# New set places for the attention and word steps of a fused attention and two-layer expert kernel

## The chip, the cores and the metric

The kernel runs on 1 core of one Trainium2 chip. The metric is device time in microseconds (us), the median of several executions. TensorE is called PE, VectorE DVE, ScalarE ACT, GpSimd POOL; SP is the engine whose queue issues nearly all transfers here.

## The reference, cut to what matters

```
scores = q @ k^T / sqrt(64)          # 4 batches, 8 heads, 576 positions, window of 64
attn   = softmax over the window
x      = attn @ v                    # 2304 tokens x 512
a, b   = x @ w1, x @ w2              # 512 -> 1024
h      = (a * b) @ w3 @ w_out        # 1024 -> 1024 -> 512
g      = leaky_relu(h @ w_in)        # 512 -> 2048
out    = g @ w_out2                  # 2048 -> 512
```

The weights arrive as 64-bit floats. "Word" stands below for one unit of 128 x 512 weights that is brought from 64 to 32 bits and then split.

## The kernel before, in words

Every large product is made of three fp32r products of high and low halves (`mm3`). The program has a first part written slot by slot, and a second part that a scheduler lays out.

**Slots.** From the start to the end of batch 2 the order on every engine is the order of the code (`Strict.on`). `slot()` issues, for the running slot number, first the attention work for PE (`ev["pe"]`), then one `ab_step`, which is 12 matmuls `ab` of 288 columns, then the eviction of the slot before, and then the other engines' work (`ev["post"]`) by rank. The first 13 slots (`HEAD`) have no `ab_step`: they hold the attention of batch 0. Batch b then takes 32 slots (`START[b]` and on), beside which the attention of batch b+1 runs. Even products are copied by ACT (`io<-ab`), odd ones multiplied on DVE (`p<-ab,io`).

**A pair.** Attention goes in 24 pairs, six to a batch: `prep` transposes q and k on DVE (six pieces for every three pairs), `scores` are 48 small matmuls `mm` on PE, `maxima` six fused operations on DVE (`s<-mm,mask`) with their read-outs, `exps` six on ACT, `normal` a sum and a product on POOL with a reciprocal on DVE between them, `turn` six transposes on PE (`mm<-ident,s`), `turned` their copies to `pts` (on DVE for batch 0, on ACT after that), `av` 24 matmuls `pa`, and then x is split by ACT (`x_hi`) and DVE (`x_lo`). `PAIRS` has the slot t of each pair's scores, and `plan()` sets the rest by fixed distances: exps at t+1, normal at t+2, turn at t+4, av at t+5, `x_lo` at t+6, with hh=1 one slot later in batch 0. Scores of a pair of batch 1 to 3 take all four banks of `ps_mm`; a turn takes two of them.

**A word.** `advance` moves four words on by one step each: scale and low bits on ACT (`f<-raw`, `low<-raw`), shift and the joining of bits on DVE (`f<-f,low`, `f<-raw,f`), then the cast to the high half on ACT (`w<-f`) and the low half on POOL (w1, w2) or DVE (the others). The load of word n+4 is queued on SP when word n's bits are joined (`feed`). Words of w1 and w2 are taken in slots 1 to 31, those of w_in and w_out beside batches 1 and 2. The rest (w3, and half of w_in) comes with batch 3.

**Fold.** Beside batch 3, w3 @ w_out is made once: a word of w3 is transposed on PE (`pa<-ident,f`), split (`w3T`), and multiplied (`mm<-wf,w3T`, 512 columns). Words of w_in are written out to DRAM by `keep` (`wd<-f`) from the buffer `f`, of which there are four for words of w3 and w_in together. From 380 us on, the remaining products run.

Of the kernel before, what the change touches and what calls it, by code (L numbers as in the profile page):

```python
# [21 lines left out]
def tile_kernel(ctx: ExitStack, tc: tile.TileContext, q, k, v, w1, w2, w3, w_out, w_in, w_out2, out):  # L22
# [18 lines left out]
    P = 128  # L41
# [18 lines left out]
    RAW = 4  # L60
    HEAD = 13
    LEAD = 13
# [105 lines left out]
    def load(ls):  # L168
        for dst, src in ls:
            sp.dma_start(dst, src)  # L170
# [154 lines left out]
    def low_bits(u):  # L325
        n_of["low"] += Strict.on
        u["low"] = (att if n_of["low"] % 2 else stage).tile([P, UC], I32, name="low", tag="low", bufs=1)
# [3 lines left out]
    def advance(stop):  # L331
# [12 lines left out]
        if now["fin"] < now["bits"]:  # L344
            u = units[now["fin"]]
            u["fin"](u["f"])
            n_of["fin"] += 1
# [127 lines left out]
    def plan():  # L475

        done = {}
        for b in range(B):
            order = [(2 * b + quad, gr) for quad in range(2) for gr in range(NG)]
            if b == 0:  # L480
                order = [(quad, gr) for gr in range(NG) for quad in range(2)]
            for (m, gr), t in zip(order, PAIRS[b]):
                at(t, 3 if b else 0, scores, m, gr, pe=True)
                for hh in range(2):
                    g = (m, hh, gr)
                    at(t, 3, maxima, g)
                    at(t + 1 + (0 if b else hh), 4, exps, g)
                    at(t + 2 + (0 if b else hh), (0, 6.5)[hh] if b else 0, normal, g)
                    at(t + (4 if b else 3 + hh), 1, turn, g, pe=True)
                    at(t + (4 if b else 3 + hh), 1, turned, g)  # L490
                    at(t + 5, 2, av, g, pe=True)
                    at(t + 5, 2, x_hi, g)
                    at(t + 6, 1, x_lo, g)
                    done[2 * m + hh] = t + 5
                if gr == 0:
                    for i in range(2 * EP):
                        if m == 1:
                            at(i // 3, 2 if i < 2 else 5, prep, m, i)
                        elif m:
                            at(t - 3 + i // 2, 5, prep, m, i)  # L500
                    if 2 <= m < 2 * B - 2:
                        at(t + 1, 7, lambda m: load(loads_qk(m)), m + 2)
# [4 lines left out]
        for t in [1, 3, 5, 7, 9, 10, 11, 13, 14, 15, 16, 17, 19, 21, 23, 25, 27, 29, 31]:  # L507
            at(t, 6, advance, PHASE_B)
        for b, stop in ((1, WO_FROM), (2, W3_FROM)):
            for i, t in enumerate(PAIRS[b + 1]):  # L510
                for d in (0, 2, 4) if i % NG < 2 else (0, 4):
                    if t + d < START[b] + 4 * KF:
                        at(t + d, 6, advance, stop)

# [13 lines left out]
    def start_loads():  # L528

        todo = [x for n in range(NHP) for x in loads_v(n)]  # L530
        for m in range(2):
# [15 lines left out]

    def ab_step(b, hf, f, j):
        cs = slice(NH * hf, NH * hf + NH)
        p, c = divmod(f, 2)  # L550
# [15 lines left out]
    def b_out(b, hf, p, c, ps, a):  # L566
        if c == 0:
            prods[p, hf] = gp.tile([P, 2, NH], F32, name="p32", tag="p32", bufs=4)
        p32 = prods[p, hf][:, c]
        with nullcontext() if Strict.on else first():  # L570
            dve.tensor_tensor(out=p32, in0=ps, in1=a, op=ALU.mult)
        if c and hf:
            p1, p2 = (prods.pop((p, i)) for i in range(2))
# [9 lines left out]
            later(3, lambda: sp.dma_start(pb[b][:, 4, p], t3))  # L583
        elif c:
            p1 = prods[p, hf]
            later(1, lambda: sp.dma_start(pb[b][:, 0:2, p], p1))
# [247 lines left out]
    for b in range(B):  # L834
        if b == 0:
            seq = [(hf, f) for fs in (range(0, 4), range(4, 8)) for hf in range(2) for f in fs]
        else:
            seq = [(hf, f) for p in range(KF // 2) for hf in range(2) for f in (2 * p, 2 * p + 1)]
# [403 lines left out]
```

## Time and profile before

| | us |
|---|---|
| median of 3 executions | 831.95 (831.71 to 832.5) |
| the profiled execution, its own time | 833.16 |
| span of the profiled execution | 831.4 |
| PE busy | 788.5 (95%) |
| DVE busy | 611.8 (74%) |
| ACT busy | 456.7 (55%) |
| POOL busy | 101.3 (12%) |

The span is from the first to the last instruction of one execution; its own time has the launch around it too. A busy share is a mean over stages with different limits, so the stages are read apart: the head and batches 0 to 2, to 272 us; batch 3 with the fold, to 380 us; and the rest. In a row of the timeline the bracket at the end is the idle time of the engine before that row, and who ended it.

### The profile page before, as it was taken

How to read it: one execution, taken by the hardware profiler on the slowest of the kernel's cores; microseconds unless marked ns; L12 is line 12 of the kernel's file. 1: busy time of each engine (PE TensorE's matmuls, PEld its weight loads, DVE VectorE, ACT ScalarE, POOL GpSimd, SP SyncE). 2: the span in 40 equal slices, each digit the busy share in tenths (PEclk: the TensorE clock that was granted, in tenths of full speed). 3: DMA queues.
4: the chain of work that ended last, by engine and by line, in shares of the span. 5: the costliest groups of instructions: out<-in, count | busy, mean ns of one | idle time of the engine just before them, and what ended most of it. 6: DMA issues, size and time to landing. Idle time of an engine off the chain costs nothing.

```text
span 831.4 us, 18254 instructions
## 1 busy us (share of the span) xinstructions
PE 788.5 (95%) x6856; PEld 761.0 (92%) x6856; DVE 611.8 (74%) x1446; ACT 456.7 (55%) x1103; POOL 101.3 (12%) x149
## 2 busy tenths in 40 slices
PE   3768999999989989999999999999999999999998
PEld 3557899999989978989999999999999999999997
DVE  5986636845882866758788886877667999798976
ACT  2866545544644424426556655555556766665744
POOL 1544622333222000000000000000000000000000
PEclk9979999999999999999999999999999999999999
DMA  9649547684461666535666356998898755343321
GB/s 273 210 117 307 181 129 185 192 257 113 128 190 45 222 187 193 180 103 158 199 191 213 121 190 218 313 332 306 307 340 270 241 190 160 102 153 125 106 96 57
DMA packets 121545, 157.97 MB, mean 190 GB/s; under 512 B 42736, under 2 KB 82928, under 8 KB 121456
## 3 DMA queue, kind: packets, MB, share of 16 engines
q1 hardware_dynamic: 121312, 156.66, 60.4%
q8 instruction: 54, 0.88, 0.4%
q14 instruction: 35, 0.29, 0.1%
q10 hardware_dynamic: 144, 0.13, 0.0%
HBM read 104.07 MB, written 52.69 MB: 189 GB/s over the span
## 4 chain that ended last, share of the span: by engine, by line
PE 72%; DVE 11%; DMA 9%; issue 3%; POOL 2%; ACT 2%; SPq 0%; DVEq 0%; ACTq 0%; POOLq 0%
PE pr L76 28%; PE o L76 22%; PE ab L78 12%; PE mm L78 5%; DMA wd<-f 4%; DVE f L76 2%; PE pa L78 2%; DMA raw<-in_moe_w_dram 2%; PE ab L76 2%; DVE f L78 2%; POOL s L78 1%; PE mm L76 1%; DVE s L78 1%; DMA vt<-in_v_dram 1%; DVE x L78 1%
## 5 line engine op out<-in xcount | busy, mean ns | idle before, releaser
L78 PE MATMUL ab<-x,w 128*128 128x288 f32 x1152 | 165.7, 301 | 0.0
L76 PE MATMUL pr<-yop,w 128*128 128x384 f32 x900 | 161.1, 337 | 0.0
L78 PEld LDWEIGHTS ab<-x,w 128*128 128x128 f32 x1152 | 156.5, 191 | 3.6 <-issue 3.2
L76 PEld LDWEIGHTS pr<-yop,w 128*128 128x128 f32 x900 | 157.4, 188 | 1.0 <-ACT c L76 0.9
L76 PE MATMUL o<-yop,yop 128*128 128x256 f32 x777 | 94.9, 282 | 0.0
L76 PEld LDWEIGHTS o<-yop,yop 128*128 128x128 f32 x777 | 93.6, 190 | 0.0
L76 ACT COPY c<-pr 128x384 f32<-128x384 f32 x95 | 45.1, 478 | 61.7 <-PE pr L76 55.0
L76 ACT CAST yop<-raw 128x256 fp32r<-128x256 f32 (+2 forms) x116 | 54.4, 491 | 38.3 <-PE o L76 34.5
L76 DVE TENSOR_TENSOR yop<-raw,yop 128x256 fp32r<-128x256 f32 (+2 forms) x116 | 58.2, 525 | 16.4 <-ACT yop L76 15.9
L78 ACT ACTIVATE s<-s,nm 128x128 f32<-128x128 f32 x144 | 56.0, 393 | 19.2 <-DVE nm L78 19.2
L76 ACT CAST yop<-f 128x512 fp32r<-128x512 f32 (+2 forms) x102 | 54.9, 567 | 20.1 <-DVE f L76 15.3
L76 DVE TENSOR_TENSOR yop<-f,yop 128x512 fp32r<-128x512 f32 (+2 forms) x102 | 59.3, 618 | 4.5 <-ACT yop L76 4.5
L76 DVE TENSOR_TENSOR c<-pr,c 128x384 f32<-128x384 f32 x74 | 40.8, 554 | 28.2 <-PE pr L76 15.6
L78 DVE CUSTOM_DVE_ANT_0 s<-mm,mask 128x128 f32<-128x128 f32 x144 | 32.2, 286 | 33.8 <-PE mm L78 33.8
L76 PEld LDWEIGHTS ab<-x,w 128*128 128x128 f32 x384 | 53.5, 189 | 1.8
L76 PE MATMUL ab<-x,w 128*128 128x288 f32 x384 | 55.1, 296 | 0.0
L76 PE MATMUL mm<-wf,w3T 128*128 128x512 f32 x192 | 52.3, 409 | 2.5 <-ACT w3T L76 2.5
L78 DVE TENSOR_TENSOR p<-ab,io 128x288 f32<-128x288 f32 x48 | 21.7, 453 | 36.2 <-PE ab L78 17.3
L78 ACT COPY io<-ab 128x288 f32<-128x288 f32 x48 | 19.1, 399 | 51.3 <-PE ab L78 51.2
L76 ACT ACTIVATE f<-raw 128x512 f32<-128x512 f32 x40 | 26.6, 674 | 35.4 <-DMA wd<-f 28.0
L76 PE MATMUL o<-w,yop 128*128 128x256 f32 x378 | 45.9, 282 | 0.0
L78 POOL TENSOR_TENSOR s<-s,rs 128x384 f32<-128x384 f32 x48 | 41.2, 858 | 36.2 <-DVE rs L78 34.3
(121 smaller groups left out, 1371.9 us busy)
## 6 DMA issues: line engine op xcount, KB each, us to landing
hd<-c SPq DMA_DIRECT2D x96, 192.0 KB, 4.1
raw<-hd SPq DMA_DIRECT2D x32, 512.0 KB, 3.7
raw<-in_moe_w_dram SPq DMA_DIRECT2D x28, 512.0 KB, 5.1
raw<-in_moe_w_out_dram SPq DMA_DIRECT2D x24, 512.0 KB, 5.1
pb<-p SPq DMA_DIRECT2D x32, 288.0 KB, 4.4
raw<-in_moe_w_in_dram SPq DMA_DIRECT2D x16, 512.0 KB, 4.0
wd<-f SPq DMA_DIRECT2D x32, 256.0 KB, 4.5
raw<-wd SPq DMA_DIRECT2D x30, 256.0 KB, 4.7
```

Source lines behind the costliest of these rows:

```text
L76: return f(*a, **k)
L78: r = f(*a, **k)
```

## The change

- A table `PLAN` replaces the distances written in `plan()`. It has a slot for every pair and, for each batch, the distances of exps, normal, turn, av and `x_lo`, each of the six transposes' slots, the slots of word steps, and those of three loads. In batch 0 pair 5 moves from slot 10 to 11. The turn of batch 3's pairs comes 5 slots behind the scores, where it was 4, the av 6 behind in batches 1 and 3; exps of the first half come in the slot of the scores.
- `turned` goes to ACT for all pairs.
- Of the 16 words of w1 and w2, five have no low bits from ACT (`low` 0): DVE masks them (`TENSOR_SCALAR f<-f`) and joins the low bits in one more operation. Eight are cast on DVE (`cast` 1).
- q and k of the first quad are loaded in three pieces each.
- Words of w_in that come among those of w3 get two buffers `fk` of their own, and two words of w3 are begun before batch 3.
- `THIRDS` is False, so its branches do nothing.

```diff
-    HEAD = 13
+    PLAN = {'head': 13, 'thirds': False, 'pairs': [[0, 2, 4, 6, 8, 11], [5, 7, 12, 19, 22, 27], [1, 6, 11, 18, 21, 27], [1, 5, 9, 15, 19, 25]], 'lags': [[1, 2, 2, 3, 3, 4, 5, 6], [0, 1, 2, 2, 4, 4, 6, 7], [0, 1, 2, 2, 4, 4, 5, 6], [0, 1, 2, 2, 5, 5, 6, 7]],
...
-        (act.copy if g[0] > 1 else dve.tensor_copy)(pts, grp[g])
+        (act.copy if PLAN["turned"][g[0] > 1][g[1]] else dve.tensor_copy)(pts, grp[g])
...
-            act.copy(t[:, 0, sl], f)
+            n = n_of["fin"]
+            (dve.tensor_copy if n < PHASE_B and PLAN["cast"][n] else act.copy)(t[:, 0, sl], f)
...
-            u["f"] = stage.tile([P, UC], F32, name="f", tag="f", bufs=4)
+            u["f"] = p0.tile([P, UC], F32, name="fk", tag="fk", bufs=2) if "own" in u else stage.tile([P, UC], F32, name="f", tag="f", bufs=4)
...
-                if now["scale"] < PHASE_B:
+                if now["scale"] < PHASE_B and PLAN["low"][now["scale"]]:
...
-        for m, t in ((2, 3), (3, HEAD + 4)):
+        for m, t in zip((2, 3), PLAN["loads"]):
...
-            at({4: 16, 5: done[0] + 1, 6: done[1] + 1}.get(n, done[n - 3] + 1), 7, lambda n: load(loads_v(n)), n)
+            at(max(PLAN["loads"][2], done[n - 3] + 1 if n > NHP else 0), 7, lambda n: load(loads_v(n)), n)
...
-            load(loads_qk(m))
+            ls = loads_qk(m)
+            load([(t[:, n * i:n * i + n], s[:, n * i:n * i + n]) for t, s in ls for i in range(EP)] if m == 0 else ls)
...
-            until(W3_FROM, W3_FROM)
+            while n_of["fin"] < W3_FROM or n_of["bits"] < W3_FROM + 2:
+                advance(W3_FROM + 2, W3_FROM)
```

On PE, the end of the head and the first slots with products, before, from the scores of pair 5 to the first scores of batch 1 (`kT` or `x` at 64x128):

```order
L78 MATMUL mm<-x 64x128 x24
L78 MATMUL mm<-ident,s 128x128 x6
L78 MATMUL pa<-pts,wf 64x64 x12
L78 MATMUL mm<-ident,s 128x128 x6
L78 MATMUL pa<-pts,vt 64x64 x12
L78 MATMUL ab<-x,w 128x288 x12
L78 MATMUL mm<-ident,s 128x128 x3
L78 MATMUL ab<-x,w 128x288 x12
L78 MATMUL pa<-pts,wf 64x64 x12
L78 MATMUL ab<-x,w 128x288 x24
L78 MATMUL mm<-kT,qT 64x128 x24
```

The same place after, from the turn that follows those scores:

```order
L79 MATMUL mm<-ident,s 128x128 x3
L79 MATMUL pa<-pts,wf 64x64 x12
L79 MATMUL mm<-ident,s 128x128 x3
L79 MATMUL pa<-pts,vt 64x64 x12
L79 MATMUL ab<-x,w 128x288 x12
L79 MATMUL mm<-ident,s 128x128 x3
L79 MATMUL ab<-x,w 128x288 x12
L79 MATMUL mm<-ident,s 128x128 x3
L79 MATMUL ab<-x,w 128x288 x12
L79 MATMUL pa<-pts,wf 64x64 x12
L79 MATMUL ab<-x,w 128x288 x24
L79 MATMUL mm<-kT,qT 64x128 x24
```

Both turns of pair 5 now stand behind the first `ab`, and five `ab` steps stand ahead of batch 1's first scores, where there were four.

On SP, the loads of words 8 to 13 (`raw`) and of v for batch 1 (`vt`, two rows a tile), before:

```order
L78 DMA raw_652<-in_moe_w1_dram 128x2x256
L78 DMA raw_717<-in_moe_w1_dram 128x2x256
L78 DMA raw_752<-in_moe_w2_dram 128x2x256
L78 DMA vt_754<-in_v_dram 128x9x64
L78 DMA vt_754<-in_v_dram 128x8x64
L78 DMA vt_757<-in_v_dram 128x9x64
L78 DMA vt_757<-in_v_dram 128x8x64
L78 DMA raw_802<-in_moe_w2_dram 128x2x256
L78 DMA raw_830<-in_moe_w1_dram 128x2x256
L78 DMA vt_832<-in_v_dram 128x9x64
L78 DMA vt_832<-in_v_dram 128x8x64
L78 DMA raw_896<-in_moe_w1_dram 128x2x256
```

After, the loads of words 8 to 14 and the first of those of v behind them:

```order
L79 DMA raw_590<-in_moe_w1_dram 128x2x256
L79 DMA raw_662<-in_moe_w1_dram 128x2x256
L79 DMA vt_664<-in_v_dram 128x9x64
L79 DMA vt_664<-in_v_dram 128x8x64
L79 DMA raw_688<-in_moe_w2_dram 128x2x256
L79 DMA raw_761<-in_moe_w2_dram 128x2x256
L79 DMA raw_796<-in_moe_w1_dram 128x2x256
L79 DMA raw_835<-in_moe_w1_dram 128x2x256
L79 DMA raw_860<-in_moe_w2_dram 128x2x256
L79 DMA vt_862<-in_v_dram 128x9x64
L79 DMA vt_862<-in_v_dram 128x8x64
```

Two of the three tiles of v went behind word 14; one went ahead of word 10.

On ACT, the first words of the fold, before (`f` is the scaled word, `w3T` the cast of a transposed one, `io` the copy of a product):

```order
L76 CAST w3T_4090<-pa_4091 128x512
L76 ACTIVATE f_4103<-raw_4086 128x512
L76 COPY io_4295<-ab_4282 128x288
L76 ACTIVATE f_4118<-raw_4101 128x512
L76 COPY io_4360<-ab_4347 128x288
L76 CAST w3T_4105<-pa_4106 128x512
L76 ACTIVATE f_4149<-raw_4116 128x512
L76 ACTIVATE f_4187<-raw_4124 128x512
L76 CAST w3T_4151<-pa_4152 128x512
L76 ACTIVATE f_4202<-raw_4162 128x512
```

After:

```order
L77 CAST w3T_4090<-pa_4091 128x512
L77 COPY io_4221<-ab_4208 128x288
L77 ACTIVATE f_4147<-raw_4114 128x512
L77 COPY io_4293<-ab_4280 128x288
L77 ACTIVATE fk_4200<-raw_4160 128x512
L77 CAST w3T_4100<-pa_4101 128x512
L77 ACTIVATE f_4185<-raw_4145 128x512
L77 COPY io_4358<-ab_4345 128x288
L77 ACTIVATE fk_4322<-raw_4263 128x512
L77 CAST w3T_4149<-pa_4150 128x512
```

Of the scaled words, those of w_in, every third of the stage, went from `f` to `fk`.

## Rows read from the trace of the kernel before

**Rows 1.** The page's head: the span.

```profile
span 831.4 us, 18254 instructions
```

**Rows 2.** PE's waits, 48 to 100 us: total us, times, longest.

```profile
PE mm L78 <- DVE qT L78: 4.1, 1, 4.1
PE mm L78 <- POOL s L78: 3.8, 4, 1.3
...
```

**Rows 3.** PE's waits, 100 to 272 us.

```profile
PE mm L78 <- POOL s L78: 3.6, 5, 1.3
PE pa L78 <- DMA vt<-in_v_dram: 0.8, 1, 0.8
PE mm L78 <- DVE qT L78: 0.7, 1, 0.7
```

**Rows 4.** PE's timeline: start, us, instructions, idle before.

```profile
45.53 0.90 PE L78 MATMUL mm<-ident,s 128*128 128x128 f32 x3 [2.59 <-DVE pts L78]
...
47.84 3.25 PE L78 MATMUL ab<-x,w 128*128 128x288 f32 x12
...
61.66 1.76 PE L78 MATMUL mm<-kT,qT 32*64 32x128 f32 x48 [4.09 <-DVE qT L78]
63.35 7.49 PE L78 MATMUL ab<-x,w 128*128 128x288 f32 x48
```

**Rows 5.** Chain that ended last, one undisturbed pair in batch 0.

```profile
106.74 0.65 PE mm L78 x6
...
108.98 0.85 PE pa L78 x24
109.83 1.07 PE mm L78 x48
110.90 6.58 PE ab L78 x48
```

**Rows 6.** Timeline of DVE and POOL in the head.

```profile
4.36 2.34 DVE L78 STREAM_TRANSPOSE kT<-x 128x384 f32<-128x384 f32 x3 [4.36 <-DMA x<-in_k_dram]
...
11.90 0.29 DVE L78 CUSTOM_DVE_ANT_0 s<-mm,mask 128x128 f32<-128x128 f32 x1 [1.61 <-PE mm L78]
...
19.15 0.29 DVE L78 CUSTOM_DVE_ANT_0 s<-mm,mask 128x128 f32<-128x128 f32 x1 [2.92 <-PE mm L78]
...
41.95 1.71 POOL L78 TENSOR_TENSOR w<-f,w 128x512 fp32r<-128x512 f32 x1
42.46 1.75 DVE L78 SCALAR_TENSOR_TENSOR f<-f,low 128x512 int32<-128x512 int32 x1
44.42 0.61 DVE L78 TENSOR_TENSOR x<-pa,x 128x192 fp32r<-128x192 f32 x2
...
48.74 0.68 DVE L78 SCALAR_TENSOR_TENSOR f<-f,low 128x512 int32<-128x512 int32 x1
```

**Rows 7.** DVE's groups, shapes apart, 0 to 272 us: busy, mean ns, idle before.

```profile
L78 DVE CUSTOM_DVE_ANT_0 s<-mm,mask 128x128 f32<-128x128 f32 x144 | 32.2, 286 | 33.8 <-PE mm L78 33.8
...
L78 DVE SCALAR_TENSOR_TENSOR f<-f,low 128x512 int32<-128x512 int32 x16 | 15.2, 948 | 0.0
...
L78 DVE TENSOR_SCALAR f<-f 128x512 int32<-128x512 int32 x16 | 9.1, 569 | 0.0
...
L78 DVE COPY pts<-mm 128x384 f32<-128x384 f32 x12 | 6.6, 547 | 2.6 <-PE mm L78 2.6
```

**Rows 8.** ACT's timeline in batch 0, the longest wait for a word.

```profile
66.92 0.67 ACT L78 ACTIVATE f<-raw 128x512 f32<-128x512 f32 x1 [5.01 <-DMA raw<-in_moe_w_dram]
```

**Rows 9.** SP's timeline: the loads of v inside those of words.

```profile
55.72 5.47 SPq L78 DMA_DIRECT2D vt<-in_v_dram  x4
```

**Rows 10.** Timeline of PE and ACT in the fold.

```profile
281.16 2.00 PE L76 MATMUL mm<-wf,w3T 128*128 128x512 f32 x8
...
295.93 0.66 ACT L76 ACTIVATE f<-raw 128x512 f32<-128x512 f32 x1 [7.42 <-DMA wd<-f]
...
297.12 3.50 PE L76 MATMUL mm<-wf,w3T 128*128 128x512 f32 x8 [2.47 <-ACT w3T L76]
```

More of the change, by code (lines that the diff above doesn't have):

```diff
@@ L60, in tile_kernel @@
     RAW = 4
-    HEAD = 13
+    PLAN = {'head': 13, 'thirds': False, 'pairs': [[0, 2, 4, 6, 8, 11], [5, 7, 12, 19, 22, 27], [1, 6, 11, 18, 21, 27], [1, 5, 9, 15, 19, 25]], 'lags': [[1, 2, 2, 3, 3, 4, 5, 6], [0, 1, 2, 2, 4, 4, 6, 7], [0, 1, 2, 2, 4, 4, 5, 6], [0, 1, 2, 2, 5, 5, 6, 7]], 'first': [0, 3, 3, 0], 'late': [[0, 4.5], [0, 0], [0, 6.5], [0, 9]], 'turns': [[0, 0, 0, 1, 1, 1], [10, 12, 15, 15, 16, 16], [25, 25, 28, 28, 30, 30], [41, 41, 43, 43, 45, 45], [56, 56, 58, 59, 62, 62], [72, 72, 73, 74, 76, 77], [86, 87, 88, 88, 89, 90]], 'turn_rank': 2, 'loads': [3, 19, 11], 'turned': [[1, 1], [1, 1]], 'words': [[0, 1, 3, 5, 7, 9, 10, 11, 12, 14, 15, 16, 17, 19, 23, 24, 26, 28, 28], [5, 6, 8, 9, 14, 14, 19, 20, 23, 23, 24], [2, 3, 4, 5, 8, 12, 14, 16, 17, 20, 20, 23, 25, 27, 27, 32, 33]], 'low': [1, 1, 1, 0, 1, 0, 1, 1, 1, 1, 1, 0, 0, 0, 1, 0], 'cast': [1, 1, 1, 1, 0, 1, 1, 0, 0, 0, 0, 0, 0, 0, 1, 1]}
+    HEAD, THIRDS = PLAN["head"], PLAN["thirds"]
     LEAD = 13
@@ L326, in low_bits, with advance @@
         n_of["low"] += Strict.on
-        u["low"] = (att if n_of["low"] % 2 else stage).tile([P, UC], I32, name="low", tag="low", bufs=1)
+        u["low"] = (att if Strict.on and n_of["low"] % 2 else stage).tile([P, UC], I32, name="low", tag="low", bufs=1)
         act.activation(out=u["low"], in_=flat(u["raw"]).bitcast(U8).rearrange("p (m e) -> p m e", e=8)[:, :, 3],
                        func=AF.Copy, scale=1.0 / 32, bias=-31.0 / 64)
-    def advance(stop):
+    def advance(stop, fins=None):
         now = dict(n_of)
@@ L460, in tile_kernel @@
             in_unit(8 + i // 2)
+            units[-1]["own"] = True
     n_of["cap"] = KEPT = len(units)
@@ L481, in plan @@
                 order = [(quad, gr) for gr in range(NG) for quad in range(2)]
-            for (m, gr), t in zip(order, PAIRS[b]):
-                at(t, 3 if b else 0, scores, m, gr, pe=True)
+            t0 = START[b - 1] if b else 0
+            for i, (m, gr) in enumerate(order):
+                t, lag = t0 + PLAN["pairs"][b][i], PLAN["lags"][b]
+                at(t, PLAN["first"][b], scores, m, gr, pe=True)
                 for hh in range(2):
@@ L495, in plan @@
[L495 to L500, printed above, removed]
+                    at(t + lag[hh], 4, exps, g)
+                    at(t + lag[2 + hh], PLAN["late"][b][hh], normal, g)
+                    at(t + lag[4 + hh], 1, turn, g, pe=True)
+                    at(t + lag[4 + hh], 1, turned, g)
@@ L501, in plan @@
+                    at(t + lag[6], 2, av, g, pe=True)
+                    at(t + lag[6], 2, x_hi, g)
+                    at(t + lag[7], 1, x_lo, g)
+                    done[2 * m + hh] = t + lag[6]
+                if gr == 0 and m:
+                    for k in range(2 * EP):
+                        at(PLAN["turns"][m - 1][k], PLAN["turn_rank"] if m == 1 else 5, prep, m, k)
                     if 2 <= m < 2 * B - 2:
-                        at(t + 1, 7, lambda m: load(loads_qk(m)), m + 2)
@@ L509, in plan @@
[L509 to L513, printed above, removed]
+            at(max(PLAN["loads"][2], done[n - 3] + 1 if n > NHP else 0), 7, lambda n: load(loads_v(n)), n)
+        for b, stop in enumerate((PHASE_B, WO_FROM, W3_FROM)):
+            for t in PLAN["words"][b]:
+                at((START[b] if b else 0) + t, 6, advance, stop + (2 if b == 2 else 0), stop)
@@ L548, in ab_step @@
     def ab_step(b, hf, f, j):
+        NH = S // (2 if b or not THIRDS else 3)
         cs = slice(NH * hf, NH * hf + NH)
@@ L566, in b_out @@
     def b_out(b, hf, p, c, ps, a):
[L567 to L572, printed above, removed]
+        for i, at_, n, n0 in ((((0, 0, 192, 0),), ((0, 192, 96, 0), (1, 0, 96, 96)), ((1, 96, 192, 0),))[hf] if b == 0 and THIRDS else ((hf, 0, NH, 0),)):
+            if (p, i) not in prods:
+                prods[p, i] = gp.tile([P, 2, NH], F32, name="p32", tag="p32", bufs=4)
+            with nullcontext() if Strict.on else first():
+                dve.tensor_tensor(out=prods[p, i][:, c, at_:at_ + n], in0=ps[:, n0:n0 + n], in1=a[:, n0:n0 + n], op=ALU.mult)
+        if c and hf == (1 if b or not THIRDS else 2):
             p1, p2 = (prods.pop((p, i)) for i in range(2))
@@ L583, in b_out @@
             later(3, lambda: sp.dma_start(pb[b][:, 4, p], t3))
-        elif c:
-            p1 = prods[p, hf]
+        elif c and hf == (0 if b or not THIRDS else 1):
+            p1 = prods[p, 0]
             later(1, lambda: sp.dma_start(pb[b][:, 0:2, p], p1))
@@ L835, in tile_kernel @@
         if b == 0:
-            seq = [(hf, f) for fs in (range(0, 4), range(4, 8)) for hf in range(2) for f in fs]
+            seq = [(hf, f) for fs in (range(0, 4), range(4, 8)) for hf in range(3 if THIRDS else 2) for f in fs]
         else:
```

18 lines of the change are left out of this document (4 added, 14 removed).

## The prediction

> **What bounds the kernel now.** I read the busy shares in slices first. Behind 380 us PE is busy in nearly every slice; nothing there is touched, so that part should only move. Everything changed lies ahead of 380 us. I then read PE's waits by stretch [rows 2, 3], PE's timeline at the places where they fall [rows 4], and the chain of waits for what an undisturbed pair costs [rows 5]: 0.65 + 0.85 + 1.07 us for turn, av and scores, and 6.58 us for four slots of products, 1.65 us a slot. Between the first product at 47.84 us [rows 4] and the end of batch 2 near 272 us stand 96 such slots (158 us), 18 whole pairs (46 us) and about 2 us left of batch 0: 206 us of work in 224 us. The 18 us between are what a better order can reach: 7.9 us of waits in the listed rows to 100 us and 5.1 us behind that [rows 2, 3], and low clock after idle time. In the head PE mostly waits, and DVE and ACT do the work one behind the other. In the fold a single wait of 2.47 us and its aftermath stand out [rows 10].
>
> **The head.** Up to the low half of x for the fourth pair, which batch 0's first product needs, the order has this on DVE: nine copies to pts fewer, four casts, two masking operations and two two-input operations on words more, and one transposition more. By the means of [rows 7] the copies give back 9 x 0.547 = 4.9 us. The added ones cost 2 x 0.95 + 2 x 0.57 = 3.0 us, and the transposition 2.34 / 3 = 0.8 us [rows 6]. A DVE cast of 512 columns has no row; the nearest is the one-input masking operation, 0.57 us, with the two-input 0.95 us as the upper bound and its undisturbed 0.68 us [rows 6] between; below 0.4 us it can hardly go. I take 0.57: 2.3 us. Net: DVE gets 1.2 us more (0.5 to 2.7). Against it stand gaps that the order now fills. The first transpositions waited for the whole of k until 4.36 us [rows 6]; with three pieces the first can start earlier, worth 0 to 1.5 us (DVE's own 2.34 us is the limit), I take 0.7. The third transposition of quad 1 falls into the idle 1.61 us before the first maxima: 0.7 us. A shift falls into the 2.92 us before the next ones [rows 6]: 0.6 us. So DVE is ready about 0.8 us earlier than 44.42 + 0.61 = 45.0 us. But PE did not start then: the turn of pair 5 stood ahead, after 2.59 us of waiting for DVE's pts [rows 4], then an av. Both turns of pair 5 now stand behind the first product, and the copies are on ACT. With the av of pair 4 still ahead I put the first product at 45.3 us: **-2.5 us** (0 to -4.0). Two things must hide for that. The first word's scale now leads ACT's queue, and the second stands between the two halves' exps of pair 0; each waits for its load, with those exps behind it. The cover is the second pair's scores and the turn of the second half, far behind; without it the wait is bounded by the longest one for a word, 5.0 us [rows 8].
>
> **Batch 0, to 100 us.** The 4.09 us for qT [rows 4] go if the six transpositions of quad 2 are done: the order starts them in slots 10 and 12, not 14, and the scores come one slot later. The pairs' other 3.8 us are turns behind POOL's product. Its cause lies on ACT: exps queued behind the scale of a word whose load came 5.01 us late [rows 8], since SP had four loads of v, 5.47 us of issuing, ahead of it [rows 9]. Now one tile of v stands ahead of word 10, two went behind word 14, and bits are joined about one slot earlier, so the loads are released earlier. Also the turn stays four slots behind the scores while the exps start one slot sooner. What is late next is word 11 or 12, with two slots (some 4.5 us) between release and scale; a wait there was carried once by the three `ab` banks: PE ran 48 products from 63.35 us without a gap [rows 4] while ACT waited [rows 8]. Of 7.9 us I leave 1.4: **-6.5 us** (-3 to -7.9).
>
> **Clock.** The scores behind the wait took 1.76 us against 1.07, the 48 products 7.49 against 6.58 [rows 4, 5]; the granted clock there was lowered after the idle time. That goes with the wait: 0.7 + 0.9 = 1.6, I take **-1.5 us** (0 to -2.5, the first twelve products took 3.25 us against 1.65 and still follow an idle PE).
>
> **Batches 1 and 2.** 3.6 us are turns behind POOL, 0.8 us an av behind a load of v, 0.7 us scores behind qT [rows 3]. Batch 3's turns get five slots in place of four, v one slot more, the transpositions are spread. Counting DVE's rows in the order, with their undisturbed durations, the worst eight slots held about 18 us of DVE work before and hold about 16 now, with about 18 us on PE. **-3.5 us** (-1 to -5.1).
>
> **Fold.** The scale of a word waited 7.42 us for a buffer f whose write to DRAM was under way; w3T and PE's 2.47 us followed, and the eight products behind took 3.50 us against 2.00 [rows 10]. With fk a word of w3 never waits for a write. That is worth 2.47 + 1.5 = 4.0 us; what remains is the load of the word itself, so I take **-3.0 us** (-1 to -4.5). Two words begun early cost batch 2 the same work that they save here: nothing.
>
> **New waits.** Four banks for scores, two for a turn: where another pair's scores stand one slot ahead of a turn (five places: slots 35, 66, 82, 86, 96), PE waits until three maxima have freed two banks, 3 x 0.286 us [rows 7] and the start on DVE, against 1.65 us of products between. That leaves 0.8 us for a late DVE. DVE sat waiting for scores 33.8 us in all [rows 7], so mostly it is not late. Bounds 0 to 5, taken **+2.0 us**. The other moves (casts and copies among ACT and DVE behind slot 17) I cost at nothing; the idle time of both engines hides them, and if it is gone the second rival below is what happens.
>
> **The sum.** -2.5 - 6.5 - 1.5 - 3.5 - 3.0 + 2.0 = -15.0 us. The profiled execution took 833.16 us with a span of 831.4 [rows 1]; it should become 818.2. It lies 1.2 us above the median of 831.95, so the median becomes **817.0 us**. With all bounds at their best it would be near 808, with all at their worst about 832.
>
> **A rule against the change.** The row first: a shift on DVE took 1.75 us at 42.46 and 0.68 us at 48.74; the long one ends just after POOL's product, itself 1.71 us, is over [rows 6]. So the two hold each other up, by up to 1.07 us. The Trainium skill, "SBUF — State Buffer", section "SBUF: two separate sides", says why: DVE and GpSimd share a pair of ports, an exclusive lock held for the whole instruction, taken by DVE operations with two SBUF inputs or in a 2-port mode. The trace agrees (1.75 against 0.68 us). By that page copies from PSUM to pts would not need the lock, while the casts that replace them do; by it I estimate that the head would keep none of its gain and the median would be 819.5 us.
>
> **Rivals.** *The words stay late* (0.15): loads of 512 KB released two slots ahead are not there, ACT holds the exps as at 66.92 us [rows 8], and batch 0 keeps its waits. For it: the word slots 14 to 17 are as dense as before. Against it: no four loads of v between. The 6.5 and 1.5 us are lost: 825.0 us.
>
> *DVE and POOL hold each other up, and it ends slower* (0.09). In the head and batch 0 DVE has 45 operations on words where it had 32. Now a shift is stretched by 0.948 - 0.68 = 0.27 us in the mean [rows 6, 7], 32 x 0.27 = 8.6 us. If the mean hold rises to 0.6 us, it is 27 us, 18.4 more, all on the engine that sets the head's end: -15.0 + 18.4 = +3.4, or 835.4 us. It decides from a mean hold of about 0.52 us on. For it: 1.07 us in one row. Against it: DVE has slack behind slot 30, and fewer words fall on the same slot.
>
> *The time comes back* (0.06): the part behind 380 us turns out to be set by transfers or DVE and starts no earlier for it: 832 us. Against it: PE has no idle slice there.
>
> **How the numbers follow.** My forecast has 0.70. Faster holds it and the first rival: 0.84 with a little taken off for their worse ends. Slower is the second rival and a mishap besides: 0.10. Same 0.06; 0.2% is about what a measurement of this kernel tells from no change. The range reaches from 809, nearly all bounds at their good end, over the first rival to 827.0.
>
> **What would show it.** The first `ab` on PE at 45.3 us, not 47.84; no wait of PE for qT before batch 1's first scores; ACT's longest wait for a word under 3 us; no wait of ACT for the transfer of wd in the fold, and eight products near 2.0 us; POOL's product and DVE's shifts no longer than now. It is wrong if the first product starts no earlier, if DVE's mean shift passes 1.2 us, or if PE's waits between 48 and 272 us still sum to over 9 us.

## The result and the profile after

The changed kernel takes 823.33 us (median of 4 executions, 821.40 to 823.52) against 832.05 us (831.71 to 832.5) for the kernel before in the same comparison: a ratio of 0.989 with a 95% interval of 0.9872 to 0.9907, or 8.7 us less. The prediction said 817.0. The profiled execution itself took 823.33 us, with this span, to be set beside [rows 1]:

```profile
span 821.5 us, 18278 instructions
```

The span is 9.9 us shorter. Where they went is seen in a view that cuts each trace at three places: PE's first product `ab`, 100 us, the end of batch 2, and the end of the fold (the first `pr`). Columns: stretch, its length, then busy time of PE, PEld, DVE, ACT and POOL with instruction counts, the granted clock of PE, the DMA share and GB/s. Before:

```profile
0.00:47.84 47.84, 25.59 (x441) 20.43 (x441) 35.55 (x127) 27.52 (x99) 21.25 (x41) 0.90 0.74 221
47.84:100.00 52.16, 44.09 (x527) 40.84 (x525) 38.54 (x94) 32.22 (x91) 25.60 (x28) 0.93 0.71 206
100.00:271.60 171.60, 166.53 (x2067) 158.99 (x2059) 101.95 (x361) 86.63 (x306) 52.66 (x80) 1.00 0.57 161
271.60:379.22 107.62, 104.69 (x643) 94.78 (x641) 75.19 (x144) 40.42 (x81) 1.79 (x2) 0.98 0.54 167
```

After:

```profile
0.00:49.76 49.76, 22.98 (x439) 18.72 (x439) 38.50 (x126) 29.89 (x102) 21.98 (x39) 0.85 0.75 215
49.76:100.00 50.24, 45.60 (x554) 42.56 (x553) 39.25 (x111) 28.41 (x94) 26.02 (x28) 0.98 0.74 220
100.00:265.77 165.77, 163.79 (x2037) 155.84 (x2035) 104.90 (x354) 85.17 (x302) 53.92 (x80) 1.00 0.57 167
265.77:369.20 103.43, 102.74 (x642) 93.39 (x641) 73.15 (x141) 39.52 (x79) 1.94 (x2) 1.00 0.53 168
```

Length less PE's busy time is PE's idle time. Four things are to be read:

- The head is 49.76 - 47.84 = 1.9 us *longer*.
- From the first product to the end of batch 2 it takes 50.24 + 165.77 = 216.0 us, where it took 223.8: 7.75 us less. PE's idle time fell from 8.07 to 4.64 us up to 100 us and from 5.07 to 1.98 us behind it, 6.5 us together; its busy time fell by 1.2 us, with the granted clock of the first stretch at 0.98 instead of 0.93.
- The fold takes 4.2 us less: 2.2 us less idle, 2.0 us less busy, at a granted clock of 1.00 instead of 0.98.
- What is left behind it is 821.5 - 369.20 = 452.3 us, and was 831.4 - 379.22 = 452.2 us. That part only moved.

1.9 - 7.75 - 4.2 + 0.1 = -9.9 us.

**The head.** PE's timeline after (start, us, instructions, idle before), to be set beside [rows 4] and the row of before that follows it:

```profile
45.44 0.90 PE L79 MATMUL mm<-ident,s 128*128 128x128 f32 x3 [4.75 <-POOL s L79]
48.28 1.55 PE L79 MATMUL pa<-pts,vt 128*64 128x64 f32 x24 [1.94 <-DVE x L79]
49.76 2.97 PE L79 MATMUL ab<-x,w 128*128 128x288 f32 x12
...
61.85 1.14 PE L79 MATMUL mm<-kT,qT 32*64 32x128 f32 x48 [1.11 <-DVE qT L79]
```

```profile
42.05 0.90 PE L78 MATMUL mm<-ident,s 128*128 128x128 f32 x3 [2.44 <-POOL s L78]
```

No turn of pair 5 is left ahead of the first product, as the order showed, and the wait of 2.59 us for pts is gone with it. But the turn of pair 4's second half waits 4.75 us for POOL's normalized `s`, where it waited 2.44 us before, and the av behind it waits 1.94 us for DVE's x. POOL's timeline after says why the turn waits:

```profile
39.20 1.28 POOL L79 TENSOR_TENSOR w<-f,w 128x512 fp32r<-128x512 f32 x1
40.84 1.64 POOL L79 TENSOR_TENSOR w<-f,w 128x512 fp32r<-128x512 f32 x1 [0.36 <-DVE w L79]
42.57 0.28 POOL L79 TENSOR_SCALAR rs<-sm 128x3 f32<-128x3 f32 x1
44.27 1.11 POOL L79 TENSOR_TENSOR s<-s,rs 128x384 f32<-128x384 f32 x1 [1.42 <-DVE rs L79]
```

Two low halves of words, 1.28 and 1.64 us, stand ahead of the `rs` and `s` that PE waits for, where one stood before. The table puts the second there: `late` of batch 0 is `[0, 4.5]`, so the second half's normalization has rank 4.5 in its slot and comes behind a low half, which has rank 1; before, its rank was 0. POOL then stands 1.42 us for DVE's reciprocal (1.47 us before).

The start of the head is later too. DVE after, to be set beside [rows 6]:

```profile
3.14 1.62 DVE L79 STREAM_TRANSPOSE kT<-x 128x384 f32<-128x384 f32 x2 [3.14 <-DMA x<-in_k_dram]
...
10.84 2.34 DVE L79 STREAM_TRANSPOSE x<-x 128x384 f32<-128x384 f32 x3 [2.50 <-DMA x<-in_k_dram]
13.02 0.28 DVE L79 CUSTOM_DVE_ANT_0 s<-mm,mask 128x128 f32<-128x128 f32 x1
```

The first transposition starts at 3.14 instead of 4.36 us, as the smaller loads promise, but the first maxima start at 13.02 instead of 11.90 us, since the second quad's k is issued later and DVE stands 2.50 us for it.

**To the end of batch 2.** PE's waits after (total us, times, longest), 46 to 100 us and 100 to 266 us, to be set beside [rows 2, 3]. The wait of 1.9 us for x lies ahead of the first product:

```profile
PE mm L79 <- POOL s L79: 2.7, 2, 1.7
PE pa L79 <- DVE x L79: 1.9, 1, 1.9
PE mm L79 <- DVE qT L79: 1.1, 1, 1.1
PE ab L79 <- ACT io L79: 0.8, 1, 0.8
```

```profile
PE mm L79 <- DVE nm L79: 1.3, 2, 1.0
PE mm L79 <- POOL s L79: 0.7, 1, 0.7
```

To 100 us 4.6 us are left of 7.9; behind it 0.7 us are left of 5.1, and a new kind of wait has come, 1.3 us for `nm`, the maxima that free the banks of the scores.

Of the 4.6 us, most fall at one place. ACT:

```profile
83.25 0.67 ACT L79 ACTIVATE f<-raw 128x512 f32<-128x512 f32 x1 [6.03 <-DMA raw<-in_moe_w_dram]
```

and PE right behind it:

```profile
85.92 1.87 PE L79 MATMUL ab<-x,w 128*128 128x288 f32 x12 [0.85 <-ACT io L79]
89.52 0.55 PE L79 MATMUL mm<-ident,s 128*128 128x128 f32 x3 [1.73 <-POOL s L79]
91.02 0.55 PE L79 MATMUL mm<-ident,s 128*128 128x128 f32 x3 [0.95 <-POOL s L79]
```

ACT stands 6.03 us for the last word of w1 and w2, with the exps of a pair and a copy to io queued behind. SP's queue shows where that word (the single `raw`) was:

```profile
49.85 14.98 SPq L79 DMA_DIRECT2D raw<-in_moe_w_dram  x5
64.88 7.52 SPq L79 DMA_DIRECT2D vt<-in_v_dram  x4
72.44 0.78 SPq L79 DMA_DIRECT2D wf<-in_k_dram  x1
...
74.29 0.60 SPq L79 DMA_DIRECT2D raw<-in_moe_w_dram  x1
```

It stands behind the loads of v, which moved, and behind k (and q, 73.27 us, not shown) of a quad of batch 2, which nobody needs for long (a quad is the four heads of a batch that three pairs treat).

**The fold.** The wait of [rows 10] for the transfer of `wd` is gone from ACT, but not the waiting. ACT's waits from the end of batch 2 to the end of the fold, before:

```profile
ACT f L76 <- DMA wd<-f: 28.0, 6, 7.4
```

and after:

```profile
ACT fk L77 <- DMA raw<-in_moe_w_in_dram: 24.7, 6, 5.2
```

ACT now waits for the word's own load. PE hardly feels it: its waits in that stretch sum to 0.7 us, none over 0.4, where they were 3.0 us with the 2.47 of [rows 10] among them.

### The profile page after: what moved, and what is told of

The parts are those of the page before. It is cut to its first block, busy times and chain, and to the rows that moved or that the text cites. A ratio compares the mean times of both kernels' runs of the same rounds, so it can differ in the third digit from the quotient of the medians.

```text
span 821.5 us, 18278 instructions
## 1 busy us (share of the span) xinstructions
PE 782.3 (95%) x6856; PEld 756.5 (92%) x6856; DVE 615.6 (75%) x1448; ACT 452.8 (55%) x1101; POOL 103.9 (13%) x149
## 4 chain that ended last, share of the span: by engine, by line
PE 85%; DVE 6%; DMA 4%; issue 2%; ACT 2%; POOL 1%; SPq 0%; DVEq 0%; POOLq 0%; ACTq 0%
PE pr L77 31%; PE o L77 22%; PE ab L79 16%; PE ab L77 5%; PE mm L77 4%; PE mm L79 4%; DVE f L79 2%; PE pa L79 2%; DMA raw<-in_moe_w_in_dram 1%; DMA wf<-in_k_dram 1%; DMA x<-in_k_dram 1%; DVE x L79 1%; PE pa L77 1%; POOL s L79 1%; ACT s L79 1%
## 5 line engine op out<-in xcount | busy, mean ns | idle before, releaser
L77 PE MATMUL mm<-wf,w3T 128*128 128x512 f32 x192 | 50.6, 400 | 0.0
L77 PEld LDWEIGHTS o<-w,yop 128*128 128x128 f32 x378 | 45.4, 191 | 0.0
L77 PE MATMUL o<-yop 128*128 128x256 f32 x357 | 44.8, 283 | 0.0
L77 PE MATMUL pr<-oh,wf 128*128 128x288 f32 x276 | 44.2, 295 | 0.0
```

The source lines that it names most:

```text
L77: return f(*a, **k)
```

## The experiments

Each is an edit of the kernel after, unless it says that it is one of the kernel before. The stages of all profiled executions in us, cut as above; "PE idle" is the sum of PE's waits in the fold; the ratio is to the kernel before on the same chip.

| kernel | first product | to end of batch 2 | fold | PE idle | span | median | ratio (95%) |
|---|---|---|---|---|---|---|---|
| before | 47.84 | 223.8 | 107.6 | 3.0 | 831.4 | 832.05 | |
| after | 49.76 | 216.0 | 103.4 | 0.7 | 821.5 | 823.33 | 0.9890 (0.9872 to 0.9907) |
| after, once more | 49.33 | 216.5 | 103.9 | 1.1 | 823.3 | 824.45 | 0.9882 (0.9858 to 0.9906) |
| sums of pair 4 first | 47.35 | 216.7 | 104.3 | 1.4 | 821.0 | 823.09 | 0.9851 (0.9827 to 0.9874) |
| q, k in one load | 49.16 | 213.5 | 102.9 | 0.3 | 817.4 | 823.64 | 0.9856 (0.9832 to 0.9881) |
| casts on ACT | 49.27 | 212.9 | 103.9 | 1.2 | 818.9 | 821.45 | 0.9837 (0.9816 to 0.9859) |
| old split of engines | 48.38 | 217.6 | 103.9 | 1.0 | 822.1 | 821.16 | 0.9831 (0.9809 to 0.9853) |
| no own buffers | 48.64 | 213.6 | 104.0 | 0.8 | 818.4 | 822.41 | 0.9851 (0.9825 to 0.9878) |
| no early words | 49.50 | 214.5 | 104.9 | 2.0 | 820.9 | 823.36 | 0.9873 (0.9851 to 0.9894) |
| old places, batches 1 to 3 | 49.26 | 221.1 | 103.2 | 0.3 | 826.4 | 829.12 | 0.9927 (0.9903 to 0.9950) |
| before + own buffers | 47.49 | 223.9 | 106.0 | 2.4 | 830.6 | 832.49 | 0.9974 (0.9957 to 0.9991) |
| before + early words | 47.77 | 222.1 | 107.3 | 3.3 | 830.2 | 833.19 | 0.9991 (0.9975 to 1.0008) |
| k, q later | 49.05 | 211.7 | 104.5 | 1.5 | 818.6 | 819.55 | 0.9816 (0.9795 to 0.9838) |
| three edits together | 46.81 | 213.9 | 104.3 | 1.2 | 819.1 | 817.79 | 0.9813 (0.9789 to 0.9837) |

How far one profile can be trusted is in the table too. The two profiles of the kernel after and the one without own buffers run the same order up to the end of batch 2, and show 216.0, 216.5 and 213.6 us for the second column, 49.76, 49.33 and 48.64 us for the first. A difference of 3 us there, or 1 us in the head, shows nothing by itself.

### What makes the head late

**Sums of pair 4 first.** In batch 0 the normalization of each pair's second half goes ahead of the words again.

```diff
-'late': [[0, 4.5], [0, 0], [0, 6.5], [0, 9]]
+'late': [[0, 0], [0, 0], [0, 6.5], [0, 9]]
```

> Undoes one number of the table: in batch 0 the normal step of a pair's second half goes back ahead of the low halves of words (rank 0 in place of 4.5). Theory (POOL's queue): in the changed kernel two low halves of words (39.20 and 40.84 us on POOL) stand ahead of the sum of pair 4's second half (42.57), PE waits 4.75 us for its product and the first product comes at 49.76 us, 1.9 later than before. With the sum first, that wait shrinks to under 2 us, the first product comes near 47.5 us and the span is about 2.3 us shorter (near 819.2, time near 821.0). Rival (DVE casts hold POOL and DVE up against each other): the wait only moves to the next low half, the first product comes no earlier than 49.0 us, the span is at most 0.7 us shorter.

PE's timeline of this kernel:

```profile
42.26 0.55 PE L79 MATMUL mm<-ident,s 128*128 128x128 f32 x3 [0.33 <-POOL s L79]
45.87 1.55 PE L79 MATMUL pa<-pts,vt 128*64 128x64 f32 x24 [3.06 <-DVE x L79]
47.35 2.59 PE L79 MATMUL ab<-x,w 128*128 128x288 f32 x12
...
59.91 1.14 PE L79 MATMUL mm<-kT,qT 32*64 32x128 f32 x48 [1.67 <-DVE qT L79]
```

The wait of 4.75 us for POOL is 0.33 us, the turn starts 3.2 us earlier, and the first product 2.0 to 2.4 us earlier than in the two profiles of the kernel after. So POOL's queue is what held the turn. But 1.1 us of it goes into a longer wait for DVE's x (3.06 us in place of 1.94), and batch 1's first scores then wait 1.67 us for qT. That x ends at 45.72 us, behind three steps on words, the first of them this one; and ACT's copy of the turn to pts, which av needs as well, ends at 45.57 us:

```profile
42.40 1.58 DVE L79 SCALAR_TENSOR_TENSOR f<-raw,f 128x512 int32<-128x512 int32 x1
...
45.10 0.47 ACT L79 COPY pts<-mm 128x384 f32<-128x384 f32 x1
```

So with POOL's order put back the first product is only where the kernels before have it (47.35 against 47.49 to 47.84 us). The median, 823.09 us, cannot be told from 823.33 and 824.45.

**q, k in one load.** The three pieces are one load again.

```diff
-            load([(t[:, n * i:n * i + n], s[:, n * i:n * i + n]) for t, s in ls for i in range(EP)] if m == 0 else ls)
+            load(ls)
```

> q and k of the first quad in one load each again. Theory (loads in thirds push what is queued behind them on SP): the second quad's transpositions wait for k until 10.84 us and the first word until 13.62 us in the changed kernel, as SP issues them 1.9 us later; with one load each the transpositions come at about 9.2 us, the first maxima at 11.9 instead of 13.02, the first product 0.8 us earlier (49.0), the span 0.8 us shorter. Rival (that time has slack by 39 us, POOL's queue decides): first product within 0.3 us of 49.76, span within 0.3.

The first maxima start at 12.15 us, 0.9 us earlier than after; the first product stands at 49.16 us, inside what repeats show, and the time is the same. The later start of the head has slack; the loads in pieces neither help nor harm.

**Casts on ACT.** All sixteen casts leave DVE.

```diff
-'cast': [1, 1, 1, 1, 0, 1, 1, 0, 0, 0, 0, 0, 0, 0, 1, 1]
+'cast': [0, 0, 0, 0, 0, 0, 0, 0, 0, 0, 0, 0, 0, 0, 0, 0]
```

> All sixteen casts of w1 and w2 on ACT again, everything else as in the changed kernel. Rival of the POOL queue theory (casts on DVE hold the ports against POOL): in the head the casts took 0.40 to 1.33 us, POOL's low half 1.64 us; without them DVE is ahead by 2 us and the first product comes near 47.8 us, the span is about 2 us shorter. Theory (order on POOL's queue): the two low halves still stand ahead of the sum, ACT gets 4 x 0.6 us more in the head, and the first product is within 0.7 us of 49.76.

DVE and POOL do hold each other up. In the kernel after, one cast of the same shape took 1.33 us beside POOL's low half of 39.20 us, and 0.41 us without one; a masking operation beside the next low half took 1.49 us:

```profile
39.43 1.33 DVE L79 CAST w<-f 128x512 fp32r<-128x512 f32 x1
...
41.28 1.49 DVE L79 TENSOR_SCALAR f<-f 128x512 int32<-128x512 int32 x1
...
48.78 0.41 DVE L79 CAST w<-f 128x512 fp32r<-128x512 f32 x1
```

Yet with no cast on DVE the first product stands at 49.27 us, where it was: the two low halves on POOL still come ahead of the sum. So the casts are not what made the head late. Whether the hold had a part in it was not tried, since without casts other steps of DVE are held. Right ahead of the x for which PE's av waits 1.94 us stands the same long step in the kernel after:

```profile
45.85 1.75 DVE L79 SCALAR_TENSOR_TENSOR f<-raw,f 128x512 int32<-128x512 int32 x1
```

and with the casts on ACT, where av waits 1.94 us as well:

```profile
45.36 1.75 DVE L79 SCALAR_TENSOR_TENSOR f<-raw,f 128x512 int32<-128x512 int32 x1
```

Both run beside a low half on POOL (1.71 and 1.63 us); without one this step takes 0.68 us. By these rows an estimated 1.1 us of that wait is the hold.

**Old split of engines.** Casts and all low bits on ACT, the copies to pts of the first two quads' pairs on DVE, as before; only the places are new.

```diff
-'turned': [[1, 1], [1, 1]]
+'turned': [[0, 0], [1, 1]]
...
-'low': [1, 1, 1, 0, 1, 0, 1, 1, 1, 1, 1, 0, 0, 0, 1, 0]
+'low': [1, 1, 1, 1, 1, 1, 1, 1, 1, 1, 1, 1, 1, 1, 1, 1]
...
-'cast': [1, 1, 1, 1, 0, 1, 1, 0, 0, 0, 0, 0, 0, 0, 1, 1]
+'cast': [0, 0, 0, 0, 0, 0, 0, 0, 0, 0, 0, 0, 0, 0, 0, 0]
```

> The division of work among ACT and DVE as in the kernel before (casts and low bits on ACT, pts copies of batch 0 on DVE), with the new places. If the new division is what lengthens the head, the first product comes at 47.8 us or earlier. If the places (POOL's queue) do, it stays within 1 us of 49.76. Batches 0 to 2 from there: if the new division helps there, 216.2 us from the first product to the end of batch 2 grow by 1 us or more; if only the places help, they stay within 0.5.

48.38 us to the first product, 821.16 us in all. The stage behind takes 217.6 us, 1.4 us over the 216.2 of the expectation, but the head is shorter by about as much: batch 2 ends at 266.0 us, where the kernel after ends it at 265.8 and 265.9. The new split brings nothing here. It may even cost some 2 us: both kernels with old casts were below the kernel after (821.45 and 821.16 against 823.33 and 824.45), and the interval of the old split, up to 0.9853, ends just below both of the kernel after (from 0.9858 on). They ran in another comparison, and their profiles show no stage that would carry it, so that stays open.

### What the new places and the loads are worth

**Old places in batches 1 to 3.** The slots of pairs, the lags, the transpositions and words of batches 1 and 2, and batch 3's places, as before; batch 0 as after.

```diff
-'pairs': [[0, 2, 4, 6, 8, 11], [5, 7, 12, 19, 22, 27], [1, 6, 11, 18, 21, 27], [1, 5, 9, 15, 19, 25]]
+'pairs': [[0, 2, 4, 6, 8, 11], [4, 8, 13, 18, 23, 28], [1, 6, 11, 17, 22, 27], [0, 5, 10, 15, 20, 25]]
...
-'turns': [[0, 0, 0, 1, 1, 1], [10, 12, 15, 15, 16, 16], [25, 25, 28, 28, 30, 30]
+'turns': [[0, 0, 0, 1, 1, 1], [14, 14, 15, 15, 16, 16], [28, 28, 29, 29, 30, 30]
...
```

> The changed kernel with the places of batches 1 to 3 (pairs, distances, transpositions, words beside batches 1 and 2) as the kernel before had them; head, words of w1 and w2, division of work, loads and fk as changed. Theory (the places of batches 1 to 3 give most of the 7.7 us gained between the first product and the end of batch 2): PE's wait for qT near 60 us (4.1) and POOL's products come back, that stretch grows from 216.2 to 222 us or more, time near 829. Rival (it is the earlier words and loads that give it): within 2 us of 216.2.

PE's waits of this kernel, 100 to 270 us, are those of [rows 3] again, less the load of v (0.8 us for qT come beside this row):

```profile
PE mm L79 <- POOL s L79: 2.9, 5, 1.4
```

From the first product to the end of batch 2, the waits for POOL's `s` sum to 5.7 us and those for qT to 2.9 us, where the kernel after has 3.4 and 1.1. That stretch takes 221.1 us against 216.0 and 216.5, and the median is 829.12 us against 823.33 and 824.45: the new places of these batches carry about 5 of the 8 us of that stage, mostly in the way that was predicted, by the turns behind POOL and the transpositions.

**k, q later.** The load of k and q that stands ahead of the last word is issued six slots later.

```diff
-at(PLAN["turns"][m - 1][-1] + 2, 7, lambda m: load(loads_qk(m)), m + 2)
+at(PLAN["turns"][m - 1][-1] + (8 if m == 2 else 2), 7, lambda m: load(loads_qk(m)), m + 2)
```

> The loads of q and k of quad 4 come 6 slots later (slot 24 in place of 18), behind word 15. Theory (what is left in batch 0 is ACT's 6.03 us wait at 83.25 us for the load of word 15, which stands on SP behind those 1.2 MB; exps stand behind it, PE waits 1.73 + 0.95 us for POOL at 89 to 91 us and 0.85 for ACT): ACT's wait falls under 3 us, those waits of PE go to under 1.5 us in sum, span 2 us shorter. Rival (transfers are busy anyway and the wait moves on to the next word): span within 0.7 us of 821.5.

SP's queue of this kernel, the load of the last word:

```profile
71.34 0.41 SPq L79 DMA_DIRECT2D raw<-in_moe_w_dram  x1
```

ACT:

```profile
76.28 0.68 ACT L79 ACTIVATE f<-raw 128x512 f32<-128x512 f32 x1 [0.36 <-DMA raw<-in_moe_w_dram]
```

and all of PE's waits from the first product to 100 us:

```profile
PE mm L79 <- DVE qT L79: 0.4, 1, 0.4
```

The word is issued at 71.34 instead of 74.29 us and used at 76.28 instead of 83.25: 2.95 us come from the issue, the other 4.0 us from a load that landed sooner, and why it did is not shown. The waits for POOL and io are gone with it. In the profiles with the new places and this load in its old place, the waits of this stretch sum to 1.0 to 4.6 us, so the profile alone would not settle it. The stage takes 211.7 us, the median is 819.55 us. The ratio's interval, 0.9795 to 0.9838, lies wholly below both of the kernel after (from 0.9858 on). The medians differ by 3.8 and 4.9 us from those of the kernel after (823.33 and 824.45), about what the waits at the place sum to: 0.85 + 1.73 + 0.95 = 3.5 us.

### What shortens the fold

Two parts of the change act there: the buffers `fk`, and the two words of w3 begun before batch 3. They were taken away from the kernel after and added to the kernel before, one at a time.

**No own buffers.**

```diff
-            units[-1]["own"] = True
```

> The changed kernel without the buffers fk: words of w_in share the four buffers f with those of w3 again. Theory (the write to DRAM of a word of w_in holds the buffer a word of w3 needs): ACT waits for a transfer of wd again, PE idles 2 to 3 us in the fold, and the fold takes about 107 us where it takes 103.4; time 827. Rival (the two words begun early, or the new start of batch 3, give the gain): the fold stays within 1 us of 103.4.

**Before + own buffers** (an edit of the kernel before).

```diff
-            u["f"] = stage.tile([P, UC], F32, name="f", tag="f", bufs=4)
+            u["f"] = p0.tile([P, UC], F32, name="fk", tag="fk", bufs=2) if "own" in u else stage.tile([P, UC], F32, name="f", tag="f", bufs=4)
...
+            units[-1]["own"] = True
```

> The kernel before with the buffers fk alone. Theory: the fold takes 103.5 to 104.5 us instead of 107.6, everything else as before; time near 828.4. Rival (the words begun early matter as much): 106 us or more, time 830 or more.

**No early words.**

```diff
-                at((START[b] if b else 0) + t, 6, advance, stop + (2 if b == 2 else 0), stop)
+                at((START[b] if b else 0) + t, 6, advance, stop, stop)
...
-            while n_of["fin"] < W3_FROM or n_of["bits"] < W3_FROM + 2:
-                advance(W3_FROM + 2, W3_FROM)
+            until(W3_FROM, W3_FROM)
```

> The changed kernel with fk but without the two words of w3 begun ahead of batch 3. New theory of the fold (the gain comes from the two words begun early: fk only moves ACT's wait from the write of wd to the load of the word, and PE does not feel it with two words in hand): the fold takes 105.5 us or more where it takes 103.4 to 104.0. Old theory (fk gives the gain): it stays at 103.4 to 104.0.

**Before + early words** (an edit of the kernel before).

```diff
-        if now["fin"] < now["bits"]:
+        if now["fin"] < min(now["bits"], fins or KEPT):
...
-                        at(t + d, 6, advance, stop)
+                        at(t + d, 6, advance, stop + (2 if b == 2 else 0), stop)
...
-            until(W3_FROM, W3_FROM)
+            while n_of["fin"] < W3_FROM or n_of["bits"] < W3_FROM + 2:
+                advance(W3_FROM + 2, W3_FROM)
```

> The kernel before with two words of w3 begun ahead of batch 3 and nothing else. New theory of the fold: 103.5 to 104.5 us, where before has 107.6, and the time about 3 us shorter. Old theory (fk needed): 106.5 us or more.

Without `fk` ACT waits for the writes again, five times and 17.8 us in all, yet the fold stays at 104.0 us: the buffers are not what shortens it in the kernel after. Without the early words it takes 104.9 us, 1.0 to 1.5 us more than in the two profiles of the kernel after and 0.4 us more than in the slowest fold of the kernels that keep both (104.5 us). Neither median, 822.41 and 823.36 us, can be told from that of the kernel after. Added to the kernel before, the buffers alone bring 107.6 - 106.0 = 1.6 us and the early words alone 0.3 us, with one wait of 3.35 us for w3T still standing at 312.35 us. So the expectation that the buffers carry the gain failed, and so did the one that the early words do.

Both together in old places bring 4.5 us (103.2 us, the kernel with old places in batches 1 to 3, whose batch 0 and split of engines are those of the kernel after). No single part does that, and with new places either can be missed at a cost of 1.5 us of fold at the most. What goes with the fold's length in all rows of the table is the column beside it: with PE waiting 0.3 us for w3T the fold takes 102.9 to 103.2 us, with 2.0 us 104.9, with 2.4 to 3.3 us 106.0 to 107.6. The new places with neither part were not run, nor was it tried which other edit of the kernel after (batch 3's places, say) stands in for one that is missing.

### The kernel once more, and three edits together

The kernel after ran again, for a comparison on the same chip, beside a kernel with three of the edits above: one load, the sums first, k and q later.

> The changed kernel as it is, once more beside the others of this call. First product, batches 0 to 2 and fold differ by up to 2.5 us between executions of equal programs up to there (batches 0 to 2 took 216.0 us in the first profile, 213.6 in the run without fk, whose program is the same in that stretch); this run says how much of the others' differences that is. Expected: time 0.984 to 0.990 of before, the first product at 48.6 to 49.8 us, the fold 103.4 to 104.

> The changed kernel with three edits together: loads of the first quad whole, the sum of a pair's second half ahead of low halves in batch 0, q and k of quad 4 loaded in slot 24. If the gains are on one path in different stretches, they add: head 2.4 to 3 us shorter than in the changed kernel (first product near 46.8), batches 0 to 2 near 212 us, time some 5 us shorter than the changed kernel of this call. If the later stretch takes back what the head gains (as with the first of the three edits alone, whose batches 0 to 2 took 216.7 us), the gain is 2 us or less over the late loads alone.

In that comparison the kernel after took 824.45 us (822.28 to 826.63), the three edits 817.79 us (817.09 to 820.87); no execution of the one reaches the other. This beats both kernels of the case. PE in the combination:

```profile
59.93 1.14 PE L79 MATMUL mm<-kT,qT 32*64 32x128 f32 x48 [1.90 <-DVE qT L79]
```

Its first product is 2.2 us earlier than with k and q later alone (46.81 against 49.05), but batch 1's first scores start only 0.4 us earlier (59.93 against 60.32), after a wait of 1.90 us for qT, and batch 2 ends at 260.7 us in both. The two medians hardly differ either (ratios 0.9813 and 0.9816). In the six profiles whose first product starts between 46.81 and 49.16 us with the new places, batch 1's first scores start between 59.91 and 60.47 us. So the first product, on which the prediction's first term stood, does not set what follows. The transpositions for batch 1 do. DVE in the combination:

```profile
50.48 0.18 DVE L79 RECIPROCAL rs<-rs 128x3 f32<-128x3 f32 x1 [2.55 <-POOL rs L79]
...
58.27 1.61 DVE L79 STREAM_TRANSPOSE qT<-x 128x384 f32<-128x384 f32 x2
```

Ahead of the last two of them stand a wait of 2.55 us for pair 5's sums and then, without a gap, 7.8 us of work on x, words and transpositions (50.48 to 58.27).

## Why the prediction was right, and where it was not

The sign was right, and so was the place of the gain as a whole: all of it lies ahead of 380 us, and what follows only moved. The sum of -15.0 us became -9.9 us of span. Term by term:

| term | predicted | measured | read from |
|---|---|---|---|
| head | -2.5 | +1.9 | first product |
| waits in batch 0 | -6.5 | -3.4 | PE's idle time to 100 us |
| clock | -1.5 | -1.2 | PE's busy time to the end of batch 2 |
| waits in batches 1 and 2 | -3.5 | -4.4 | old kinds of wait, 5.1 to 0.7 |
| fold | -3.0 | -4.2 | its length |
| new waits | +2.0 | +1.3 | waits for `nm` |

Head, batch 0 and clock came out 7.8 us worse than forecast, the other three terms 2.8 us better. That the time still lies in the range owes something to these misses of opposite sign and to the width of the range; one of the prediction's own signs of being wrong, a first product that starts no earlier, did appear.

- **Head: the step that failed.** It summed DVE's queue and set the first product where DVE would be ready, with PE's av still ahead. It did not walk POOL's queue: there the order had two low halves of words, not one, ahead of the sum for pair 4's second half, and PE's turn waits for that sum. That is worth 2.0 to 2.4 of the 4.5 us between the forecast of 45.3 and 49.76 us. The rest lies in the sum itself. With POOL's order put back the first product stands at 47.35 us: DVE's x, forecast for 45.0 - 0.8 = 44.2 us, ends at 45.72 us there, ACT's copy to pts, which had no price, at 45.57 us, and the av takes 1.55 us, where 1.1 us were left for it. The bounds (0 to -4.0) had excluded a loss for no stated reason. A further error lies under it, which the runs show: the gain asked for would not have carried to batch 1, where a first product ahead of 49.2 us moved the first scores by 0.6 us at the most.
- **Batch 0: mis-sized.** -6.5 us became -3.4. The long wait for qT is down from 4.1 to 1.1 us, and the words that the text watched, 11 and 12, cost no PE wait. But it left 1.4 us and 4.6 us remained. The rival in which the words stay late came true in part, but some eight slots further on, at the last word; its cause is a load of k and q ahead of it on SP. The text followed the loads of v past the words, and not these. With them moved the waits behind the first product are 0.4 us, so what the term promised was there to be had.
- **Clock, batches 1 and 2, new waits: as predicted.** Scores and products behind the first twelve take 1.14 us and 3.43 us (24 products) in the kernel after, where [rows 4] have 1.76 us and 7.49 us (48 products). Scores ahead of a turn did make PE wait for the maxima, at two of the five places.
- **Fold: the size nearly, the mechanism by half.** PE's wait for w3T and the slow products behind it are gone, as said. But `fk` moved ACT's wait from the write to the load rather than ending it; in old places it took a lead of words as well, which the prediction had costed at nothing.
- **DVE and POOL.** The rival that ends slower needed a mean hold of 0.52 us. DVE's groups, shapes apart, 0 to 266 us, to be set beside [rows 7]:

```profile
L79 DVE TENSOR_SCALAR f<-f 128x512 int32<-128x512 int32 x24 | 16.5, 687 | 1.3 <-ACT f L79 1.3
...
L79 DVE SCALAR_TENSOR_TENSOR f<-f,low 128x512 int32<-128x512 int32 x10 | 9.1, 912 | 0.0
```

The shift went from 948 to 912 ns, the masking from 569 to 687 ns, far from it. The Trainium skill's rule ("SBUF — State Buffer", section "SBUF: two separate sides") gave the right outcome for the head, no gain kept. The lock shows in the rows (0.41 against 1.33 us), but taking the casts off DVE, to which the estimate put it down, left the first product where it was; the order on POOL's queue accounts for 2.0 to 2.4 us, and what the holds of DVE's other steps cost the head is open.

The median fell 1.2 us less than the span, because the profiled execution of before lay about 1.1 us above its median and that of the kernel after lies at its own. The prediction took the same distance off both kernels, so this, too, is part of the miss: 5.1 us of span and 1.2 us of this make the 6.3 us between 817.0 and 823.33.

## What to carry to other kernels

When a table moves work, walk the queue of every engine that the step on the path depends on, the little used ones too: here one more operation of POOL, an engine that is 13% busy, came between PE and a sum it needed. On a queue that issues loads in order, ask of each load who needs it first and when; one that stands far ahead of its use, in front of one that is used at once, is a wait in the making; moving it gave the lowest median of the single edits here. And ask of every milestone whether the next thing is really counted from it: a first product 2.2 us earlier moved the next scores by 0.4 us, since DVE's transpositions set them.

## What the runs showed of the chip

A load's issue can hold SP's queue for very different times. SP in the kernel after, early in the head:

```profile
4.47 0.43 SPq L79 DMA_DIRECT2D wf<-in_moe_w_dram  x1
...
10.49 3.00 SPq L79 DMA_DIRECT2D wf<-in_moe_w_dram  x1
```

The issue of one word took 0.43 us, that of the next of the same size 3.00 us, and that of two loads of v between them 5.50 us (4.95 us, not shown); at 49.85 us five words took 14.98 us. What stands behind such a load waits with it, so the order on SP counts and not only the number of loads.

The other thing not expected is how far two executions of one order drift apart. The kernel after and the one without own buffers run the same up to batch 3, and batch 1's first scores started at 61.85 us in the one profile and at 59.91 us in the other; the medians of one kernel in two comparisons differed by 1.1 us, those of the kernel before by up to 2.9 us (832.05 to 834.90).
